# A frequency-domain convolution on one core: weight differences spread over rounds, evictions shared by clocked sums, a third range for one tile, fillers among the last matmuls

## The chip, the core and the metric

The kernel runs on one core of a Trainium2 chip. The core has a matrix engine (TensorE; the profile lists its matmuls as PE and its weight loads as PEld), VectorE (DVE), ScalarE (ACT), GpSimd (POOL) and SyncE (SP, which here only issues transfers). They run side by side and wait for each other on semaphores. The metric is device time in microseconds; a profiled execution has a span besides, from its first to its last instruction.

## The reference: what is computed

```python
# x: (1, 224, 224, 96) bf16, w: (7, 7, 96, 96) bf16
wp = jnp.pad(w, ((0, H - K), (0, W - K), (0, 0), (0, 0)))
Xf = rfft2(x, axes=(1, 2));  Wf = rfft2(wp, axes=(0, 1))
Yf = jnp.einsum('bhwi,hwio->bhwo', Xf, Wf)
y = irfft2(Yf, s=(H, W), axes=(1, 2)).astype(bf16)
```

That is a circular 7x7 convolution of a 224x224 image, with 96 input channels and 96 output channels.

## The kernel before: stages, queues and names

The width is cut into seven tiles of 32 pixels. Along the height the kernel works with short Fourier transforms of length 34 on eight blocks of 28 rows: each block becomes 17 frequency planes (`NS` = 17) of two real parts. Along the width the seven taps stay a direct convolution, with even and odd pixels apart. All matrix work is on PE, in PSUM banks of 512 columns; one pool holds all eight banks, and a bank is free again when it has been evicted (copied to SBUF).

Four kinds of work follow each other for each tile.

- **Forward transform.** Matmuls of the pixels (`xn`, for the first tile `WF`'s late end) with the transform matrix `Fm`; their evictions fill `xf`. Later tiles use `a_jobs` (all 17 planes at once, line 414). The first three tiles use `f_jobs` (line 424), which does the planes in two ranges, `SH2` = (0, 8, 17) (line 41), since the buffer of an earlier tile comes free plane by plane: `xf` has two buffers. A range has one matmul for each pixel, phase and half of the rows, 64 in all, with 2·(planes)·4 columns. `new_xf` (line 363) copies three halo pixels on ACT for each range and phase. `then_load` hangs the load of a later tile's pixels on the last job of a range.
- **Weights.** `prep_jobs(gi)` (line 320) transforms the weights of one group of planes (`PGRP`, line 31): twelve jobs `mk_` of four matmuls (`pb<-wq`, 120 columns each) with one eviction to `WF`, and then, except for the first group, one `diff` a plane (line 350): a DVE subtraction on 96x960 elements, w2 = w0 - w1, the third of the three weight planes that a complex product by three real ones needs. The jobs of a group and its differences form one list.
- **Rounds.** `b_round(t, s)` (line 474) does one plane of one tile. 33 matmuls (`pb<-WF,J` and `pb<-WF,xf`, 96 columns) go to two banks. After the first bank's, ACT makes `tt_` and DVE makes `u`; then the jobs of `mid()` are put in; after the second bank's matmuls DVE makes `v`; and POOL (or DVE, where `ydve`) adds u and v to `yf`, which goes to a scratch tensor in DRAM. The second part of the first bank's weights (slot 2 of the plane) is a difference, so a round's third group of matmuls waits for it. `jit` (line 446) makes the sums and differences `J` of `xf` on DVE for up to three planes ahead.
- **Inverse transform.** `c_jobs` (line 627): the scratch is read back as `tt`; two matmuls a job with the matrix `G` (`pb<-tt,Gm`, 384 columns), each evicted to an output tile (`yo` or a freed `J` buffer) and sent out.

The first two tiles run together, the second four rounds behind (`LAG`), in a loop over r from 0 to 20 (line 739); their rounds share the time with the weights of all groups and with the third tile's forward transform. The remaining tiles run one after the other, with the forward transform of the next and the inverse of the one before between their rounds.

The order is the program's own: every engine runs its instructions in the order in which they are written down. `add(a, b, jobs)` (line 723) gives a list of jobs the slots a to b (two slots a round, so slot k belongs to round k/2), and `pace` (line 707) draws from each list evenly. Every transfer keeps its place too. Almost all instructions are recorded through one helper, so the profile gives L87 for nearly every line; groups are told apart by tile names.

`evac` (line 122) chooses DVE or ACT for an eviction: it keeps a running sum of estimated costs for each (`load["v"]`, `load["a"]`), to which rounds, `jit` and `diff` add their own, and takes the engine whose sum stays lower. The sum of DVE starts at `BIAS` = 3000 (line 703).

**The end** (from line 825). The last tile's scratch is in six parts with own loads (`load_p`); a first block of its inverse (planes 0 to 8, matrix `GA`, function `first`) needs only early parts, the second (`GB`, function `second`) adds the planes from the last three and ends the bank. Seven jobs, 14 matmuls, of the tile before remain and run ahead; then eight `first` matmuls take all eight banks, then `WARM` = 20 matmuls with zeros from the tile `wu` are added to the last bank (line 847), then `second` and `first` alternate, each `second` evicted by DVE and ACT in turn (`tail_evac`) and sent out two by two. The last write to scratch is issued by ACT, and the two loads that wait for the scratch parts by SP ahead of the last output transfers.

Of the kernel before, what the change touches and what calls it, by code (L numbers as in the profile page):

```python
# [14 lines left out]
B = 28  # L15
# [12 lines left out]
NTAP = 10  # L28
# [9 lines left out]
JGB = ((0, 3), (3, 6), (6, 9), (9, 12), (12, 15), (15, 17))  # L38
LAG = 4
CQ = {2: (11, 0), 3: (11, 2), 4: (9, 4), 5: (7, 5), 6: (6, 4)}  # L40
SH2 = (0, 8, 17)
MERGE = ()
NP2 = 0
WARM = 20
BIAS = 3000.0


def slot(s, part):
# [4 lines left out]
def kernel(  # L53
# [7 lines left out]
    _, H, W, C = x.shape  # L61
# [6 lines left out]
    FR = 2 * NS  # L68
# [39 lines left out]
    def bank():  # L108
        return pools["psb"].tile([128, 512], F32, name="pb")

    load = {"v": 0.0, "a": 0.0}
    tail = [0]
    parts = {}

# [7 lines left out]
    def evac(out_ap, in_ap, n):  # L122
        if tail[0]:
            return tail_evac(out_ap, in_ap, n)
        cv, ca = 180 + 1.0 * n, 160 + 0.85 * n
        if load["v"] + cv <= load["a"] + ca:
            load["v"] += cv
            return VE.tensor_copy(out=out_ap, in_=in_ap)
        load["a"] += ca
        return SE.copy(out=out_ap, in_=in_ap)  # L130
# [189 lines left out]
    def prep_jobs(gi):  # L320
        s0, s1 = PGRP[gi]
        ns = s1 - s0
        full = gi == 0
        ncol = (NSLOT_OF(s0, s1) if full else 2 * ns) * NTAP
        nb = C // NB
        hb = NB // 2
        assert NB * ncol <= 512 and C2 % hb == 0

        def mk_(ob):
            def f():  # L330
                pw = bank()
                pv_ = pw[:, 0:NB * ncol].rearrange("p (k h q) -> p k h q", h=2, q=ncol)
                ev = Em[:, :, slot(s0, 0):slot(s1 - 1, 2) + 1, :]
                ev = ev.rearrange("p h a t -> p h (a t)") if full else ev.rearrange("p h (s r) t -> p h s (r t)", r=3)[:, :, :, 0:2 * NTAP]
                for k in range(hb):
                    o = ob * hb + k
                    TE.matmul(pv_[:, k], lhsT=wqx[0:PW2, o:o + 127 * C + 1:C], rhs=ev, start=True, stop=True)
                pv_ = pv_[0:C]
                o0, o1 = ob * hb, (ob + 1) * hb
                wv = WF[0:C, slot(s0, 0):slot(s1 - 1, 2) + 1]  # L340
                if full:
                    wv = wv.rearrange("i a t (h o) -> i (a t) h o", h=2)
                    apart(("W", gi), ob, evac(wv[..., o0:o1], pv_.rearrange("i k h q -> i q h k"), NB * ncol))
                    return
                wv = wv.rearrange("i (s r) t (h o) -> i s (r t) h o", r=3, h=2)
                apart(("W", gi), ob, evac(wv[:, :, 0:2 * NTAP, :, o0:o1],
                      pv_.rearrange("i k h (s q) -> i s q h k", s=ns), NB * ncol))
            return f

        def diff(s):  # L350
            def f():
                load["v"] += 60 + C * NTAP / 1.92
                w0, w1, w2 = (WF[0:C, slot(s, r)].rearrange("i t o -> i (t o)") for r in range(3))
                VE.tensor_tensor(out=w2, in0=w0, in1=w1, op=ALU.subtract)
            return f
        return [mk_(ob) for ob in range(nb)] + ([] if full else [diff(s) for s in range(s0, s1)])

    def NSLOT_OF(s0, s1):
        return slot(s1 - 1, 2) + 1 - slot(s0, 0)
# [24 lines left out]
        apart(("A", t), (pos, jg, ph), evac(xo, pi, m * FR * JG))  # L384

    def a_mm(pa, xb, px, n):
        for k in range(n):
            i = px + 2 * k
            TE.matmul(pa[:, k * FR * JG:(k + 1) * FR * JG], lhsT=xb[:, i * C:i * C + 128],
                      rhs=Fm.rearrange("p r s j -> p (r s j)"), start=True, stop=True)  # L390
# [31 lines left out]
        return jobs  # L422

    def f_jobs(t, part):
        s0, s1 = SH2[part], SH2[part + 1]
        n = 2 * (s1 - s0) * JG
        nr = -(-TW * n // 512)
        e = [-(-TW * i // nr) for i in range(nr + 1)]
        fv = Fm[:, :, s0:s1].rearrange("p r s j -> p r (s j)")

        def mk_(jg, a, b, ph):
            def f():
                pa = bank()
                for k in range(b - a):
                    i = 2 * (a + k) + ph
                    TE.matmul(pa[:, k * n:(k + 1) * n], lhsT=xbuf(t, jg)[:, i * C:i * C + 128], rhs=fv, start=True, stop=True)
                xo = xf_tiles[t][0:C, ph, :, s0:s1, HALO + a:HALO + b, jg * JG:(jg + 1) * JG]
                pi = pa[0:C, 0:(b - a) * n].rearrange("c (w r s j) -> c r s w j", r=2, s=s1 - s0, w=b - a)
                return apart(("A", t), (a, jg, ph, part), evac(xo, pi, (b - a) * n))
            return f  # L440
        return [[mk_(jg, a, b, ph) for a, b in zip(e[:-1], e[1:]) for ph in range(2)] for jg in range(2)]
# [32 lines left out]
    def b_round(t, s, mid, end, ydve=False, planes=()):  # L474
# [14 lines left out]
        def conv(bank, col, m, part, add=False, both=False):  # L489
            pl = st[m][part] if s > 0 else (xv[:, 0, :, 0], Jb[:, 2:4], Jb[:, 0:2])[m][:, part]  # L490
            tp = TAPS[m]
            for k, tp_ in enumerate(tp):
                o, wv = bank[:, col:col + C], WF[0:C, slot(s, part), tp_, :]
                if both:
                    o, wv = bank[:, col:col + 2 * C].rearrange("p (m o) -> p m o", m=2), wv.unsqueeze(1).to_broadcast([C, 2, C])
                TE.matmul(o, lhsT=pl[:, (HALO - k) * NJ:(HALO - k) * NJ + 128], rhs=wv,
                          start=(k == 0 and not add), stop=(k == len(tp) - 1 and not both and m != 2 or not add and not both and k == len(tp) - 1))
# [19 lines left out]
        else:  # L517
# [39 lines left out]
                if last is not None:  # L557
                    tc.add_manual_dep(y.ins, last.ins.name, SYNC, reason="sum after planes")
            load["a"] += 490 if merge else 410
            load["v"] += (560 if ydve else 350 if t < 2 else 0) + (560 if merge else 900)  # L560
            end()
        if s == y1 - 1:
            dst, yo0 = scr_tiles[t], 0
# [63 lines left out]
    def c_jobs(t):  # L627
        jobs = []
        w0 = t * 2 * TW
        for gi, h in LT:  # L630
            hold = {}
            nq = 2 if gi < 2 else 3

            def mk_(q, gi=gi, h=h, nq=nq, hold=hold):
                def put(j0, nj, px, npx, row, col):
                    dma(out[0, j0 * B:(j0 + nj) * B, w0 + px:w0 + px + npx, :].rearrange("h w c -> h (w c)"),
                        hold["yo"][row:row + nj * B, col:col + npx * C])

                def f():
                    if q % 2 == 0:  # L640
                        hold["yo"] = new_yo()
                    tt = tt_tiles[(t, gi, h)]
                    yo = hold["yo"]
                    nj = 2 if q == 2 else 3
                    for b in range(2):
                        pb = bank()[0:nj * B, 0:4 * C]
                        TE.matmul(pb, lhsT=G[0:nj * FR, 0:nj * B],
                                  rhs=tt[0:nj * FR, 4 * q + 2 * b:4 * q + 2 * b + 2, :].rearrange("p w e -> p (w e)"), start=True, stop=True)
                        k = 2 * (q % 2) + b
                        evac(yo[0:nj * B, k * 4 * C:(k + 1) * 4 * C], pb, 4 * C)  # L650
                    if q == 1 and gi < 2:
                        put(gi * 3, 3, h * PXC, PXC, 0, 0)
                    elif q == 1:
                        put(6, 2, 0, 16, 0, 0)
                        for j in range(2):
                            put(6 + j, 1, 24, 8, 2 * B, j * 8 * C)
                    elif q == 2:
                        put(6, 2, 16, 8, 0, 0)
                    if q == nq - 1:
                        held[gi == 2] -= 1  # L660
                        pump()
                return f
            for q in range(nq):
                jobs.append(mk_(q))
# [23 lines left out]
            f()  # L688
    for _ in range(3):
        warm(9)  # L690
    for f in prep_jobs(0):
        f()
    last = [f() for f in fj[0][1]]
    for jg in range(2):
# [5 lines left out]
    stmp_cm.__exit__(None, None, None)  # L700
    yf_pool = ctx.enter_context(tc.tile_pool(name="yf", bufs=YBUF))
    tv_pool = ctx.enter_context(tc.tile_pool(name="tv", bufs=2))
    load["v"], load["a"] = BIAS, 0.0

    t_pool = t2_pool = yo_pool = None

# [17 lines left out]
        qs.append([a, b, jobs, len(jobs)])  # L724

    for gi in range(1, len(PGRP)):
        add(2 * PGRP[gi - 1][0], 2 * PGRP[gi - 1][1] - 1, prep_jobs(gi))
    for t in range(2):
        scr_tiles[t] = dr_pool.tile([TW, NJ, NS, 4 * C], BF16, name="scr")
    bursts = {}  # L730
# [8 lines left out]
    for r in range(NS + LAG):  # L739
        if r == 0:  # L740
            add(0, 4, fj[1][1])
        for p in range(2):
            if r == (1, 3)[p]:
                new_xf(1, SH2[p], SH2[p + 1])
                fj = f_jobs(1, p)
                if p == 1:
                    for jg in range(2):
                        fj[jg][-1] = then_load(fj[jg][-1], 2, jg)
                add(2 * r + 1, 2 * r + (5, 8)[p], fj[0] + fj[1])
        for p in range(2):  # L750
            if r == (9, 17)[p]:
                new_xf(2, SH2[p], SH2[p + 1])
                fj = f_jobs(2, p)
                if p == 1:
                    for jg in range(2):
                        fj[jg][-1] = then_load(fj[jg][-1], 3, jg)
                add(2 * r, 2 * r + (10, 6)[p], fj[0] + fj[1])
        if r == PGRP[-2][1] + 1:
            assert not any(q[2] for q in qs[:len(PGRP) - 1])
            wtmp_cm.__exit__(None, None, None)  # L760
            t_pool = ctx.enter_context(tc.tile_pool(name="tt", bufs=NTT, side="right"))
            t2_pool = ctx.enter_context(tc.tile_pool(name="tt2", bufs=1, side="right"))
# [130 lines left out]
```

## Time and profile before

| | |
|---|---|
| time, median of 5 runs | 277.16 us (275.04 to 280.5) |
| profiled execution: time, span | 278.79 us, 277.1 us |
| PE busy, PEld busy | 261.0 us (94%), 238.3 us (86%) |
| DVE, ACT, POOL busy | 221.9, 195.3, 98.0 us |
| bytes moved | 46.76 MB, mean 169 GB/s |
| granted TensorE clock, mean | 0.986 |
| chain that ended last | PE 59%, DVE 13%, issue 8%, DMA 7%, ACT 6% |

The page is of one execution. "Busy" sums the time with at least one instruction in work; matmuls overlap, so a busy PE is not a PE at its peak. A row of the timeline gives the start, the duration, the engine, the operation with output and input, and in brackets the engine's idle time before it with what ended it; neighbouring instructions of the same kind are merged into one row with their number (x12). A number such as 0.50 for the clock is the share of full speed that was granted. The stages that matter below are: up to 18 us loads and tables; 18 to about 104 us the first two tiles with the weights; to 257 us the other tiles; then the end.

### The profile page before, as it was taken

What the parts mean: (1) busy time and instruction counts of PE and PEld (TensorE: products, weight loads), DVE (VectorE), ACT (ScalarE), POOL (GpSimd) and SP (SyncE); (2) the same over time, 40 slices, a digit from 0 to 9 for tenths busy, and PEclk for the clock granted to TensorE, in tenths of its full rate; (3) what the DMA queues carried; (4) which work ended last, traced back from release to release, by engine and by line L of the source; (5) the groups of instructions that cost most, each with busy time, mean ns of one, the idle gap of its engine ahead of it and who ended that gap; (6) DMA issues with size and microseconds to landing.
All of it is one profiled execution on the core that took longest, in us unless ns stands there. A gap on an engine that the chain in (4) does not pass through costs nothing.

```text
span 277.1 us, 11903 instructions
## 1 busy us (share of the span) xinstructions
PE 261.0 (94%) x5018; PEld 238.3 (86%) x5018; DVE 221.9 (80%) x464; ACT 195.3 (70%) x478; POOL 98.0 (35%) x146
## 2 busy tenths in 40 slices
PE   8969898999999899999999999999999999988893
PEld 3649898999999898899999999999999999978572
DVE  5528789998979869977977897888988799988923
ACT  5428896859782676897988879887988864445413
POOL 7720022246446553233243224223323416323000
PEclk9998999999999999999999999999999999999989
DMA  7945213151111199995969487777957642898656
GB/s 186 211 113 148 67 47 107 45 150 47 45 48 67 71 285 148 259 280 158 306 186 260 124 233 210 204 228 181 309 167 192 198 154 89 200 237 245 191 160 195
DMA packets 46609, 46.76 MB, mean 169 GB/s; under 512 B 35274, under 2 KB 37974, under 8 KB 46458
## 3 DMA queue, kind: packets, MB, share of 16 engines
q1 hardware_dynamic: 45692, 44.34, 58.1%
q10 hardware_dynamic: 864, 1.67, 1.8%
q8 instruction: 39, 0.64, 1.0%
q14 instruction: 14, 0.11, 0.1%
HBM read 24.65 MB, written 21.33 MB: 166 GB/s over the span
## 4 chain that ended last, share of the span: by engine, by line
PE 59%; DVE 13%; issue 8%; DMA 7%; ACT 6%; POOL 3%; SPq 1%; DVEq 0%; ACTq 0%
PE pb L87 59%; DMA wq<-in_w_dram 5%; DVE J L87 4%; DVE v L87 3%; POOL yf L87 3%; DVE WF L87 2%; DMA out_dram<-J 2%; ACT WF L87 2%; ACT xf L87 2%; DVE u L87 2%; DVE yf L87 1%; SPq L87 1%; ACT J L87 1%; DVE yo L87 0%; DVE xf L87 0%
## 5 line engine op out<-in xcount | busy, mean ns | idle before, releaser
L87 PE MATMUL pb<-WF,J 96*128 96x96 bf16 x2898 | 166.2, 206 | 5.1 <-ACT yo L87 1.4
L87 PEld LDWEIGHTS <-J 96*128 96x128 bf16 x2898 | 141.7, 98 | 14.1 <-issue 5.3
L87 POOL TENSOR_TENSOR yf<-v,u 128x384 bf16<-128x384 f32 x85 | 84.6, 1012 | 147.3 <-issue 100.4
L87 ACT CAST xf<-pb 96x408 bf16<-96x408 f32 (+4 forms) x146 | 68.1, 494 | 8.2 <-PE pb L87 4.8
L87 PE MATMUL pb<-WF,xf 96*128 96x96 bf16 x952 | 60.2, 206 | 1.6 <-DVE WF L87 1.2
L87 DVE TENSOR_TENSOR J<-xf 96x1824 bf16<-96x1824 bf16 (+1 forms) x84 | 59.2, 744 | 0.1
L87 PEld LDWEIGHTS <-xf 96*128 96x128 bf16 x952 | 47.1, 98 | 2.1 <-issue 1.7
L87 PE MATMUL pb<-Fm,xn 118*128 118x136 bf16 (+2 forms) x512 | 43.0, 208 | 0.2 <-DVE u L87 0.2
L87 ACT CAST WF<-pb 96x480 bf16<-96x480 f32 (+1 forms) x59 | 29.2, 577 | 8.2 <-PE pb L87 8.1
L87 PE MATMUL pb<-tt,Gm 102*84 102x384 bf16 (+1 forms) x132 | 32.3, 326 | 1.2 <-DVE yo L87 0.7
L87 ACT CAST yo<-pb 84x384 bf16<-84x384 f32 (+1 forms) x62 | 26.6, 483 | 5.9 <-PE pb L87 3.8
L87 ACT CAST J<-pb 84x384 bf16<-84x384 f32 (+1 forms) x63 | 27.1, 487 | 4.6 <-DMA tt<-scr 2.6
L87 PEld LDWEIGHTS <-xn 118*128 118x128 bf16 x512 | 27.8, 98 | 0.6 <-issue 0.4
L87 DVE TENSOR_TENSOR J<-J 96x912 bf16<-96x912 bf16 (+1 forms) x42 | 25.0, 595 | 0.0
L87 PE MATMUL pb<-wq 98*128 98x120 bf16 (+1 forms) x288 | 22.0, 230 | 2.3 <-DMA wq<-in_w_dram 2.3
L87 PEld LDWEIGHTS <-wq 98*128 98x128 bf16 x288 | 20.0, 150 | 2.8 <-issue 2.7
L87 PE MATMUL pb<-wu 128*128 128x512 bf16 (+1 forms) x64 | 16.9, 431 | 1.0 <-DVE ct L87 1.0
L87 DVE TENSOR_TENSOR yf<-v,u 128x384 bf16<-128x384 f32 x27 | 15.7, 580 | 0.9
L87 PEld LDWEIGHTS <-wu 128*128 128x128 bf16 (+1 forms) x64 | 8.1, 128 | 9.0 <-issue 3.5
L87 DVE CAST WF<-pb 96x480 bf16<-96x480 f32 (+1 forms) x13 | 7.5, 610 | 8.2 <-PE pb L87 8.1
L87 PEld LDWEIGHTS <-Gm 102*84 102x84 bf16 (+1 forms) x132 | 11.3, 117 | 3.1 <-issue 2.2
L87 DVE TENSOR_TENSOR WF<-WF 96x960 bf16<-96x960 bf16 x15 | 10.9, 777 | 0.0
(393 smaller groups left out, 233.7 us busy)
## 6 DMA issues: line engine op xcount, KB each, us to landing
scr<-yf SPq DMA_DIRECT2D x30, 288.0 KB
xn<-in_x_dram SPq DMA_DIRECT2D x12, 672.0 KB
tt<-scr SPq DMA_DIRECT2D x24, 336.0 KB
out_dram<-yo SPq DMA_DIRECT2D x12, 252.0 KB
out_dram<-J SPq DMA_DIRECT2D x12, 252.0 KB
tt<-scr SPq DMA_DIRECT2D x6, 288.0 KB
wq<-in_w_dram SPq DMA_DIRECT2D x1, 1719.0 KB
scrl<-yf ACTq DMA_DIRECT2D x5, 288.0 KB
```

Source lines behind the costliest of these rows:

```text
L87: r = fn(*a, **k)
```

## The change

It has five parts.

1. `prep_jobs` returns the weight jobs and the differences apart. The jobs keep the group's slots; each difference gets its own slot, 2(s - 1) for plane s, the middle of the round before the one that uses it.
2. The sums of `evac` get a clock: `load["p"]` adds up an estimate of PE's time wherever matmuls are written down, and both sums are raised to it before each choice. Some estimates change too (a difference 250 + 500 for 60 + 500; a round on POOL 150 for 350), and `BIAS` is 2000.
3. `SH2` becomes a table by tile. The third tile's planes are done in three ranges (0, 8, 13, 17), begun in rounds 9, 14 and 17, in place of two begun in 9 and 17.
4. Behind each of the 14 inverse matmuls at the end stands one matmul with zeros into the same bank (384 columns), which ends the bank's accumulation.
5. `WARM` is 12 in place of 20.

```diff
-SH2 = (0, 8, 17)
+SH2 = {0: (0, 8, 17), 1: (0, 8, 17), 2: (0, 8, 13, 17)}
...
-WARM = 20
-BIAS = 3000.0
+WARM = 12
+BIAS = 2000.0
...
         cv, ca = 180 + 1.0 * n, 160 + 0.85 * n
+        for k in "va":
+            load[k] = max(load[k], load["p"])
         if load["v"] + cv <= load["a"] + ca:
...
-                load["v"] += 60 + C * NTAP / 1.92
+                load["v"] += 250 + C * NTAP / 1.92
...
-        return [mk_(ob) for ob in range(nb)] + ([] if full else [diff(s) for s in range(s0, s1)])
+        return [mk_(ob) for ob in range(nb)], [] if full else [diff(s) for s in range(s0, s1)]
...
+                load["p"] += max(26.0, 0.43 * n) * (b - a)
...
+            load["p"] += 42.5 * len(tp)
...
-            load["v"] += (560 if ydve else 350 if t < 2 else 0) + (560 if merge else 900)
+            load["v"] += (560 if ydve else 150 if t < 2 else 0) + (560 if merge else 900)
...
                         TE.matmul(pb, lhsT=G[0:nj * FR, 0:nj * B],
-                                  rhs=..., start=True, stop=True)
+                                  rhs=..., start=True, stop=not tail[0])
+                        if tail[0]:
+                            TE.matmul(pb.rearrange("p (a b) -> p a b", a=3), lhsT=wu[:, 0:nj * B], rhs=wu[:].unsqueeze(1).to_broadcast([128, 3, 128]),
+                                      start=False, stop=True)
...
-        add(2 * PGRP[gi - 1][0], 2 * PGRP[gi - 1][1] - 1, prep_jobs(gi))
+        pj, dj = prep_jobs(gi)
+        add(2 * PGRP[gi - 1][0], 2 * PGRP[gi - 1][1] - 1, pj)
+        for i, f in enumerate(dj):
+            k = 2 * (PGRP[gi][0] + i) - 2
+            add(k, k + 1, [f])
...
-        for p in range(2):
-            if r == (9, 17)[p]:
-                new_xf(2, SH2[p], SH2[p + 1])
+        for p in range(3):
+            if r == (9, 14, 17)[p]:
+                new_xf(2, SH2[2][p], SH2[2][p + 1])
                 fj = f_jobs(2, p)
-                if p == 1:
+                if p == 2:
...
-                add(2 * r, 2 * r + (10, 6)[p], fj[0] + fj[1])
+                add(2 * r, 2 * r + (8, 7, 5)[p], fj[0] + fj[1])
```

More of the change, by code (lines that the diff above doesn't have):

```diff
@@ L109, in bank @@
         return pools["psb"].tile([128, 512], F32, name="pb")
-    load = {"v": 0.0, "a": 0.0}
+    load = {"v": 0.0, "a": 0.0, "p": 0.0}
     tail = [0]
@@ L334, in f @@
                 ev = ev.rearrange("p h a t -> p h (a t)") if full else ev.rearrange("p h (s r) t -> p h s (r t)", r=3)[:, :, :, 0:2 * NTAP]
+                load["p"] += 63.0 * hb
                 for k in range(hb):
@@ L386, in a_mm @@
     def a_mm(pa, xb, px, n):
+        load["p"] += 59.0 * n
         for k in range(n):
@@ L424, in f_jobs @@
     def f_jobs(t, part):
-        s0, s1 = SH2[part], SH2[part + 1]
+        s0, s1 = SH2[t][part], SH2[t][part + 1]
         n = 2 * (s1 - s0) * JG
@@ L646, in f @@
                         pb = bank()[0:nj * B, 0:4 * C]
+                        load["p"] += 166.0
                         TE.matmul(pb, lhsT=G[0:nj * FR, 0:nj * B],
-                                  rhs=tt[0:nj * FR, 4 * q + 2 * b:4 * q + 2 * b + 2, :].rearrange("p w e -> p (w e)"), start=True, stop=True)
+                                  rhs=tt[0:nj * FR, 4 * q + 2 * b:4 * q + 2 * b + 2, :].rearrange("p w e -> p (w e)"), start=True, stop=not tail[0])
+                        if tail[0]:
+                            TE.matmul(pb.rearrange("p (a b) -> p a b", a=3), lhsT=wu[:, 0:nj * B], rhs=wu[:].unsqueeze(1).to_broadcast([128, 3, 128]),
+                                      start=False, stop=True)
                         k = 2 * (q % 2) + b
@@ L690 @@
         warm(9)
-    for f in prep_jobs(0):
+    for f in prep_jobs(0)[0]:
         f()
@@ L702 @@
     tv_pool = ctx.enter_context(tc.tile_pool(name="tv", bufs=2))
-    load["v"], load["a"] = BIAS, 0.0
+    load["v"], load["a"], load["p"] = BIAS, 0.0, 0.0
     t_pool = t2_pool = yo_pool = None
@@ L743 @@
             if r == (1, 3)[p]:
-                new_xf(1, SH2[p], SH2[p + 1])
+                new_xf(1, SH2[1][p], SH2[1][p + 1])
                 fj = f_jobs(1, p)
@@ L749 @@
                 add(2 * r + 1, 2 * r + (5, 8)[p], fj[0] + fj[1])
-        for p in range(2):
-            if r == (9, 17)[p]:
-                new_xf(2, SH2[p], SH2[p + 1])
+        for p in range(3):
+            if r == (9, 14, 17)[p]:
+                new_xf(2, SH2[2][p], SH2[2][p + 1])
                 fj = f_jobs(2, p)
-                if p == 1:
+                if p == 2:
                     for jg in range(2):
                         fj[jg][-1] = then_load(fj[jg][-1], 3, jg)
-                add(2 * r, 2 * r + (10, 6)[p], fj[0] + fj[1])
+                add(2 * r, 2 * r + (8, 7, 5)[p], fj[0] + fj[1])
         if r == PGRP[-2][1] + 1:
-            assert not any(q[2] for q in qs[:len(PGRP) - 1])
+            assert not any(q[2] for q in qs[:4 * len(PGRP) - 8])
             wtmp_cm.__exit__(None, None, None)
```

## The prediction

> **What bounds the kernel now.** I read four views in this order: the table of busy time by stage, the waits of the matrix engine (PE), the timelines of the stretches where PE waits, and the fine table of the last 20 us. By stage (start:end, length, then busy us of PE, PEld, DVE, ACT, POOL, the granted PE clock, DMA share, GB/s):
>
> ```profile
> 24.00:34.00 10.00, 9.01 (x187) 8.71 (x186) 8.07 (x15) 8.78 (x22) 0.37 (x1) 1.00 0.54 145
> 34.00:50.00 16.00, 14.38 (x324) 14.02 (x321) 15.25 (x28) 13.30 (x33) 4.01 (x4) 1.00 0.23 67
> ...
> 112.00:238.00 126.00, 125.86 (x2536) 118.31 (x2533) 106.38 (x223) 103.88 (x265) 44.14 (x44) 1.00 0.73 209
> ...
> 262.00:268.00 6.00, 5.96 (x28) 4.19 (x27) 1.06 (x3) 0.95 (x3) 0.00 (x0) 0.72 0.81 225
> ```
>
> From 112 to 238 us PE is busy for 125.86 of 126 us: nothing that moves work between DVE and ACT is worth anything there. The change must earn its keep ahead of 112 us, where PE is idle for 10-9.01 + 16-14.38 = 2.6 us up to 50 us and, by the same table, 0.8 us in 80:93 (PE 12.22 of 13, DVE 11.38), and in the tail. PE's waits ahead of 112 us, apart from the first load, are 1.9 us on "DVE WF" in three pieces, 1.4 on "DVE u", 1.3 on "DVE J". The largest piece, DVE and then PE:
>
> ```profile
> 43.31 2.54 DVE L87 TENSOR_TENSOR WF<-WF 96x960 bf16<-96x960 bf16 x3
> 45.77 0.54 DVE L87 SCALAR_TENSOR_TENSOR v<-tt__944,pb 128x384 f32<-128x384 f32 x1
> ...
> 44.76 0.33 PE L87 MATMUL pb<-WF,xf 96*128 96x96 bf16 x4 [1.02 <-DVE WF L87]
> ```
>
> Three weight differences stand in one clump of 2.54 us; PE waits 1.02 us for the first, and v, which frees the sum on POOL, is queued behind all three. In the tail:
>
> ```profile
> 259.74 1.01 DVE L87 CAST yo<-pb 84x384 bf16<-84x384 f32 x2
> ...
> 262.06 1.00 DVE L87 CAST yo<-pb 84x384 bf16<-84x384 f32 x2
> ...
> 263.94 4.38 PE L87 MATMUL pb<-wu 128*112 128x384 bf16 x20
> ...
> 268.15 0.98 PE L87 MATMUL pb<-xf,GB 128*112 128x384 bf16 x5
> 268.51 4.47 DVE L87 CAST tt<-pb 112x384 bf16<-112x384 f32 x8 [5.45 <-PE pb L87]
> ```
>
> The 20 fillers on zeros (wu) take 4.38 us, and the last real matmuls (GB) begin the moment they end; DVE has waited 5.45 us. Are the fillers hiding a load? They run before the last part of the last tile (32 rows, 192 KB) must have arrived. Its write to scratch is issued by ACT at 259.85 and has landed when SP issues the read, about 261.8: 1.95 us. The read is as large, so it lands near 264.0. PE therefore has about 4 us of fillers too many. The clock in the same stretch:
>
> ```profile
> 261.50:262.00 0.50, 0.50 (x4) 0.29 (x3) 0.50 (x2) 0.50 (x2) 0.00 (x0) 1.00 0.03 8
> ...
> 262.50:263.00 0.50, 0.50 (x4) 0.30 (x3) 0.50 (x2) 0.45 (x2) 0.00 (x0) 0.50 0.99 273
> ...
> 266.00:266.50 0.50, 0.50 (x5) 0.39 (x4) 0.00 (x0) 0.00 (x0) 0.00 (x0) 1.00 0.86 258
> ```
>
> After the loosely filled stretch of inverse matmuls (257 to 262, PE busy 3.80 of 5 us) the clock falls to 0.50 until about 265.7, so first eight and most fillers run at half speed.
>
> **The tail, worked out.** The inverse matmuls left at the end are 14, each with one evacuation, 7 to an engine; DVE cannot begin them before its last yf ends (259.74), and they end at 263.06 (262.06 + 1.00). A filler behind each adds 14 x 0.163 us (from the 0.33 us of a pair spaced at 0.165) = 2.3 us of PE work and delays each evacuation by one filler; but eight PSUM banks let eight pairs run ahead of 259.74, and the other six pairs (6 x 0.33 = 2.0 us) are released from 260.3 on, so each is ready before its evacuation's turn. Cost nothing; if that lead were gone, one filler and its drain, 0.3 us. The eight "first" matmuls need the freed banks: the last can start after 263.06 and ends near 263.45. Twelve fillers at full clock: 12 x 0.163 = 1.95 us, so the GB matmuls start at 265.4, later than the landing at 264.0, and 2.75 us earlier than 268.15. From there everything is as before (24 matmuls, 16 evacuations, eight output transfers), but those transfers now meet the earlier outputs, which hold the DMA engines until about 267.2 (225 GB/s over 262:268); 8 x 172 KB at some 275 GB/s end near 272.3, against 270.97 + 1.9 by the issues (last issue ends 273.72 now). I take 0.15 us off: **-2.6**.
>
> [...] Full clock gives -2.6; half clock throughout gives 263.06 + 0.4 + 12 x 0.325 = 267.4, or -0.8. PE's share rises from 3.8 to nearly all of the first eight pairs and two thirds after; I take full clock.
>
> **Differences one per round.** The 15 differences remain (642 ns each, up to 1401 beside POOL); each now stands alone between u and v in the round before its own. Round 2's first use waits for the first difference as before, but ACT has one 360-column evacuation (0.51 us) less ahead of it, so the 0.74 us wait shrinks by about 0.5; the 1.02 at 44.76 goes; of the 0.44 us at 86.35 (a J held up behind the clump at 81.74, 2.13 us) most goes. Together 1.9 us. What is late next: DVE is full in 34:50 (15.25 of 16), evacuation work there stays, and "DVE u" keeps its 0.52 at 49.52. I keep three quarters: **-1.5**. Bounds: 0, if the stretch is simply the two engines' total work; -3.4, all idle of 24:50 and 80:93. Each v waits 0.64 us behind a difference in 15 rounds instead of about 2 us in five; POOL has room (44 of 126 us).
>
> **Clocked sums.** They only choose the engine. In the order of the changed program DVE has three evacuations more than before (xf 17 for 14, yo 5 for 4, WF 6 for 7), and after 112 us only two change engine. Three of 0.5 us, hidden under a full PE or in DVE's idle fifth: **0**; if that cover is gone, 0.5 us each, 1.5 us.
>
> **Third tile in three ranges.** Its 128 forward matmuls (64 and 72 columns) become 192 (64, 40, 32), the evacuations stay 20 (8+8+4), two ACT halo copies are added (0.16 us of fixed cost each, hidden: ACT is busy 4.76 of 13 us in 80:93). Rows: 16 matmuls of 64 columns take 0.63 us, so (0.63-0.193)/15 = 29.1 ns apart; 12 of 72 columns take 0.56, or 33.0. In proportion to columns, 40 and 32 would cost 64 x (18.2+14.6) = 2.1 us, no more than the 64 x 33.0 = 2.1 now. [...] No row is narrower than 64 columns; between 25 and 29.1 I take 27: 3.5 us, **+1.4** of PE work. Where it falls: the 40-column range sits in rounds 14 to 16 (83 to 93 us), where PE's round takes 1.60 us (83.11 to 92.69, six rounds) for 33 x 42.6 ns = 1.40 us of matmuls, because DVE sets the pace; 1.2 us of slack swallow most of its 1.7 us. The stretch after it, 93 to 100, loses 0.4 us, and the 1.42 us in which ACT waited at 101.01 to evacuate the third tile goes, and with it a good part of the 0.52 us that PE waits for J at 105.84. The fourth tile's pixel load hangs on the last of these jobs and stands one place earlier in SP's queue, ahead of a scratch write (98.91 now) that is not read for many rounds; its pixels are first used at 104.03, so the swap costs nothing, and 0.7 us of SP's issue if the write mattered. Net **0** (from -0.7 to +1.4).
>
> **Sum.** -2.6 - 1.5 + 0 + 0 = -4.1 us against the profiled execution: span 277.1 to 273.0, time 278.79 to 274.7. The runs' median is 277.16, 1.6 below the profiled one; I set the same difference against it: **273.1 us**.
>
> **Rivals.**
> 1. The first stage is bound by the total work of DVE and ACT, not by its clumps: gain there 0, and the third range costs 0.5: -2.1, 275.1. For it: DVE 15.25 and ACT 13.30 of 16 us; against: ACT sat idle 2.70 us at 43.73 to 46.43 waiting for PE.
> 2. The clock falls in spite of the fillers: tail -0.8, sum -2.3, 274.9. For it: the six later pairs still come at the pace of the evacuations.
> 3. All idle goes, and PE alone bounds from 24 us: -2.6 - 3.4 + 0.4 = -5.6, 271.6.
> 4. Slower: narrow matmuls are held by their weight loads. Each loads 128 columns anew (98 ns a load, overlapped today). [...] It decides from (2.1+1.2+4.1)/128 = 58 ns a pair. [...]
>
> **How the numbers follow.** Chances: forecast 0.48, rival 1 0.18, rival 2 0.12, rival 3 0.12, rival 4 0.10. One per cent (2.8 us, about what a measurement of this kernel can tell from no change) puts the bounds at 274.4 and 279.9. The forecast with its own range (271.8 to 274.6) is nearly always below the first; rivals 1 and 2 lie just above it and fall under it one time in four, given the 275.0 to 280.5 that runs spread now; rival 3 is below. That makes faster 0.64, same 0.28, slower 0.08. The range reaches from rival 3's lower side to above rivals 1 and 2: 270.3 to 276.7.
>
> **What would show it.** Tail: PE clock 1.00 in 262 to 266, GB matmuls some 2 us after the last wu, starting about 2.3 us after DVE's last yo evacuation (5.1 now). First stage: no "DVE WF" wait over 0.4 us, and 112 us (the third tile's first inverse matmul) reached 1 to 2 us earlier. Third tile: 32-column matmuls spaced 25 to 29 ns, rounds 14 to 16 still near 1.6 us. I am wrong if the clock shows 0.50 again, if PE idles before the GB matmuls for the load, or if "DVE u" waits replace those on WF.

## The result, and the profile after

The changed kernel takes 277.52 us (median of 36 runs, 274.61 to 280.57), the kernel before beside it 277.99 (71 runs, 274.57 to 285.3). The ratio is 1.0001 [0.9981, 1.0022]: no change. (Medians here are over all runs; the ratios leave disturbed runs out, so the two differ a little.) The forecast of 273.1 us was wrong, and its range ended 0.8 us below the result. The profiled execution of the changed kernel has a time of 279.02 us and a span of 277.2, against 278.79 and 277.1. The two profiles are not alike in clock: it is 0.50 in before from 20.12 to 23.53 and in the tail from 262.46 to 265.88, in the changed kernel from 19.86 to 26.68 and from 241.72 to 245.14.

These are the rows by stage that answer to the four shown of before (length, then busy us of PE, PEld, DVE, ACT, POOL, then clock, DMA share, GB/s), from the changed kernel:

```profile
24.00:34.00 10.00, 9.76 (x191) 9.62 (x189) 8.12 (x16) 8.41 (x20) 0.00 (x0) 0.87 0.42 118
34.00:50.00 16.00, 15.42 (x346) 15.07 (x343) 15.39 (x31) 13.97 (x35) 5.94 (x6) 1.00 0.23 68
112.00:238.00 126.00, 125.83 (x2534) 118.24 (x2532) 106.65 (x225) 101.63 (x258) 44.17 (x44) 1.00 0.74 209
262.00:268.00 6.00, 5.82 (x35) 4.09 (x34) 2.91 (x7) 2.83 (x7) 0.00 (x0) 1.00 0.75 199
```

PE is fuller up to 50 us (15.42 for 14.38 in the second row), and the tail has its full clock (1.00 for 0.72). Both are what was wanted; where did the time go? To find the place I compared the starts of all 119 `tt_`, one a round, each counted from the first weight matmul (the first weights arrive at 16.9 to 18.9 us, which differs from run to run and is nobody's doing). Changed minus before: -1.34 us at the 13th round, +1.27 at the 27th, +0.96 from the 41st to the 105th, +3.24 at the 107th, +2.81 at the last. So a gain in the first rounds is lost before round 27, and 2.3 us more go near 237 us; 1.3 of these are back at the 110th (+1.95), and 0.9 go again by the last, after the second stretch at half clock. The longer half clock at the start lies ahead of the 13th round. The kernel c4 below is the same program up to its last fillers and has none there: it stands at -3.87 at the 13th and at -1.25 at the 27th, so the 2.6 us lost between the two are no matter of the clock. The tail then gives 1.7 us back: from the last `tt_` to the end it is 17.7 us for 19.4.

The first loss, in the changed kernel's timeline (start, duration, engine, operation, output and input):

```profile
57.66 1.73 DVE L87 TENSOR_TENSOR J<-xf 96x1824 bf16<-96x1824 bf16 x2
59.31 0.62 DVE L87 TENSOR_TENSOR J<-J 96x912 bf16<-96x912 bf16 x1
59.86 0.34 DVE L87 SCALAR_TENSOR_TENSOR u<-pb,tt__1431 128x192 f32<-128x192 f32 x1
60.07 1.00 POOL L87 TENSOR_TENSOR yf<-v,u 128x384 bf16<-128x384 f32 x1 [1.95 <-issue]
60.13 1.45 DVE L87 TENSOR_TENSOR WF<-WF 96x960 bf16<-96x960 bf16 x1
61.50 0.54 DVE L87 SCALAR_TENSOR_TENSOR v<-tt__1431,pb 128x384 f32<-128x384 f32 x1
61.63 0.33 PE L87 MATMUL pb<-WF,xf 96*128 96x96 bf16 x4 [0.78 <-DVE WF L87]
```

The lone difference at 60.13 takes 1.45 us, and PE waits 0.78 us for it. It begins 0.06 us after a sum on POOL that ends at 61.07, and 61.07 + 0.51 = 61.58 is its end: nearly all of its own 0.64 us is done after the sum. Ten of the fifteen lone differences are drawn out in this way by a running sum, and each ends 0.51 to 0.52 us after it. Is the difference too long, or only too late for PE? PE came for this one at 60.85 (61.63 - 0.78); had it lasted 0.64 us, it would have ended at 60.77. The other long wait, 0.88 us at 87.09, reads the same: PE came at 86.21, and the difference begun at 85.59 would have ended at 86.23. So some 1.6 of PE's 2.4 us on differences come from their length. The other way round, POOL stood still for 1.95 us while DVE made the J: the v that its sum adds was done at 57.74, but the sum began at 60.07, 0.1 us after the last J. In these rows the two engines take turns. The groups of the two kernels (count, then busy us, mean ns, idle before), before and then changed:

```profile
L87 DVE TENSOR_TENSOR WF<-WF 96x960 bf16<-96x960 bf16 x15 | 10.9, 777 | 0.0
```

```profile
L87 DVE TENSOR_TENSOR WF<-WF 96x960 bf16<-96x960 bf16 x15 | 15.8, 1055 | 0.2
```

The same fifteen subtractions cost 4.9 us more of DVE. In before's five clumps of three only the first meets a running sum: it takes 0.99 to 1.40 us in four clumps and 0.65 in the one without a sum, and the ten behind take 0.64 to 0.65. In those four the next sum on POOL, which waits for the v behind the clump, begins 0.54 us after the clump's end.

The second loss, near 237 us (SPq and ACTq are issues of transfers):

```profile
233.05 1.22 SPq L87 DMA_DIRECT2D out_dram<-J  x3
234.37 0.33 SPq L87 DMA_DIRECT2D out_dram<-yo  x1
234.89 4.40 SPq L87 DMA_DIRECT2D tt<-scr  x6
237.99 0.34 ACTq L87 DMA_DIRECT2D scrl<-yf  x1
238.71 0.85 ACT L87 CAST yo<-pb 84x384 bf16<-84x384 f32 x2 [4.08 <-DMA tt<-scr]
239.23 0.70 PE L87 MATMUL pb<-tt,Gm 102*84 102x384 bf16 x2 [1.26 <-ACT yo L87]
```

The program makes ACT's issue of a scratch write wait for an earlier transfer whose completion counter it uses, the third `out_dram<-J`; that wait ends at 237.94, and ACT's evictions queue behind the issue (ACT idle for 4.08 us). The chain of waits names it (start, us, what): it has landed 4.0 us after its start. POOL's sums, for which the write waits too, were done at 236.20.

```profile
233.90 4.01 DMA out_dram<-J
```

The records of its counter have every increment but one by 235.78, 1.88 us after the issue, and the last at 237.91. In before the same issue stood at 236.01, when POOL's sums were done, and ACT waited 2.02 us, for PE.

### The profile page after: what moved, and what is told of

It is laid out like the page before. It is cut to its first block, busy times and chain, and to the rows that moved or that the text cites. A ratio compares the mean times of both kernels' runs of the same rounds, so it can differ in the third digit from the quotient of the medians.

```text
span 277.2 us, 12048 instructions
## 1 busy us (share of the span) xinstructions
PE 264.1 (95%) x5088; PEld 241.9 (87%) x5088; DVE 227.2 (82%) x467; ACT 196.2 (71%) x477; POOL 99.8 (36%) x146
## 4 chain that ended last, share of the span: by engine, by line
PE 63%; DVE 14%; issue 8%; DMA 6%; ACT 3%; POOL 3%; SPq 1%; DVEq 0%; ACTq 0%
PE pb L87 63%; DVE J L87 5%; DMA wq<-in_w_dram 5%; DVE WF L87 4%; POOL yf L87 3%; DVE v L87 2%; DVE u L87 2%; DMA out_dram<-J 1%; SPq L87 1%; ACT xf L87 1%; ACT WF L87 1%; DVE yf L87 1%; ACT yo L87 1%; DVE tt L87 0%; DVEq L902 0%
## 5 line engine op out<-in xcount | busy, mean ns | idle before, releaser
L87 PE MATMUL pb<-WF,J 96*128 96x96 bf16 x2898 | 168.7, 207 | 1.4 <-ACT yo L87 0.4
L87 POOL TENSOR_TENSOR yf<-v,u 128x384 bf16<-128x384 f32 x85 | 86.4, 1032 | 148.5 <-issue 98.3
L87 ACT CAST xf<-pb 96x408 bf16<-96x408 f32 (+5 forms) x143 | 67.1, 490 | 7.8 <-PE pb L87 5.7
L87 PE MATMUL pb<-WF,xf 96*128 96x96 bf16 x952 | 61.7, 207 | 2.6 <-DVE WF L87 2.1
L87 PE MATMUL pb<-Fm,xn 118*128 118x136 bf16 (+4 forms) x576 | 44.4, 203 | 0.0
L87 PE MATMUL pb<-tt,Gm 102*84 102x384 bf16 (+1 forms) x132 | 34.1, 330 | 1.3 <-ACT yo L87 1.3
L87 PE MATMUL pb<-wu 128*128 128x512 bf16 (+3 forms) x70 | 19.1, 403 | 1.0 <-DVE ct L87 1.0
L87 DVE TENSOR_TENSOR WF<-WF 96x960 bf16<-96x960 bf16 x15 | 15.8, 1055 | 0.2
L87 PEld LDWEIGHTS <-wu 128*128 128x128 bf16 (+3 forms) x70 | 8.0, 116 | 8.8 <-issue 3.5
L87 DVE CAST WF<-pb 96x400 bf16<-96x400 f32 (+1 forms) x12 | 7.0, 609 | 7.3 <-PE pb L87 7.1
```

Source lines behind the costliest of these rows:

```text
L87: r = fn(*a, **k)
```

## The experiments

Each run records its span and mean granted clock. The clock explains a good part of the scatter: over the 177 runs behind the ratios below, a fit with one constant for each kernel, one for each group of runs, and one slope gives 0.64 ± 0.10 us of span for each us of lost clock, (1 - clock) x span, and leaves a scatter of 0.8 us. "At equal clock" below is the difference from before by this fit. Over all 245 runs the slope is 0.88 ± 0.07; c1 then comes out 1.1 us lower, the others move by 0.6 us or less, and no sign changes.

| kernel | median us | ratio to before | at equal clock, us |
|---|---|---|---|
| a1_clumps: changed, differences in clumps | 275.47 | 0.9905 [0.9864, 0.9945] | -2.4 ± 0.6 |
| b1_tail: before + fillers and `WARM` 12 | 276.50 | 0.9965 [0.9936, 0.9994] | -0.3 ± 0.4 |
| b2_diffs: before + one difference per round | 279.70 | 1.0018 [0.9979, 1.0056] | +1.4 ± 0.6 |
| b3_range: before + third range | 278.79 | 0.9992 [0.9961, 1.0024] | -0.4 ± 0.5 |
| c1_after_v: changed, difference behind v | 285.45 | 1.0218 [1.0151, 1.0285] | +6.0 ± 0.8 |
| c2_sums: before + clocked sums | 277.11 | 0.9933 [0.9901, 0.9965] | -1.0 ± 0.6 |
| c3_late: a1 + late evictions as before | 274.92 | 0.9840 [0.9784, 0.9896] | -2.7 ± 0.8 |
| c4_warm: changed, `WARM` 4 | 276.85 | 0.9965 [0.9929, 1.0000] | -0.4 ± 0.6 |
| d1_lead: changed, difference behind v, earlier | 275.58 | 0.9926 [0.9899, 0.9953] | -2.7 ± 0.8 |
| d2_lead_late: d1 + late evictions as before | 274.11 | 0.9877 [0.9830, 0.9923] | -2.8 ± 0.8 |

Before had medians of 278.14 beside a and b, 279.43 beside c, 278.11 beside d. The changed kernel has no row, since no clock is on record for the runs of before beside it; c4 stands for it, as the same program but for eight fillers.

**a1_clumps.** One part undone:

```diff
-        for i, f in enumerate(dj):
-            k = 2 * (PGRP[gi][0] + i) - 2
-            add(k, k + 1, [f])
+        add(2 * PGRP[gi - 1][0], 2 * PGRP[gi - 1][1] - 1, pj + dj)
```

> The changed kernel with its differences put back into one clump of three at the end of each group's list. If lone differences are what costs (beside a sum on POOL they take 1.17 to 1.46 us, in a clump only the first does), their mean falls from 1055 to near 780 ns, round 28 comes some 1.5 us earlier counted from the first weight matmul, and the time is 1 to 2 us below the changed kernel and below before (276). If the third range is what costs, nothing changes against the changed kernel (277.5).

The ratio falls from 1.0001 to 0.9905: lone differences cost the changed kernel 2.7 us by the ratios, and 2.0 at equal clock by c4 (-0.4) against a1 (-2.4). In the profile a1's rounds stand at -1.85 us against before from the 41st on, where the changed kernel's stand at +0.96, a part of it for its 3.4 us more of half clock; mean of a difference 772 ns.

**b1_tail, b2_diffs, b3_range.** One part each, put into the kernel before, with the edits of the change itself.

> The kernel before with the end's two edits alone (fillers behind the 14 inverse matmuls, 12 for 20 behind the first eight). If the end gains what the two traces show (last yf to the end 15.6 us after the change, 17.3 before), the time is 1.5 to 2 us below before (275.8). If it is given back in the output transfers or the last load, it is within 0.5 us of before.

> The kernel before with one difference per round alone. If lone differences cost, their mean is above 1000 ns and the time is 0.5 to 1.5 us above before, with a gain up to round 12 and a loss from there to round 28. If the prediction's step was right, 1.5 us below before.

> The kernel before with the third tile's forward in three ranges alone. By the prediction 0 (within 0.7 us of before); if the third range is what ate the gain, 1 to 2 us above before, with the loss in rounds 24 to 33.

The tail gives 1.0 us (ratio 0.9965), between the two outcomes named; but little of it (0.3 ± 0.4) at equal clock: mean lost clock falls from 3.2 us in before to 2.2, which at 0.64 is the other 0.7. Lone differences are no gain even alone: their mean is 1096 ns here too, and PE's waits on "DVE WF" from 24 to 104 us rise from 1.9 us in three pieces to 4.8 in seven. The third range is free, as expected.

**c2_sums.** The edits of `evac`, its estimates and `BIAS`, put into the kernel before.

> The kernel before with the clocked sums alone (new costs and the start of DVE's sum with them). Theory, from the rounds of the changed kernel with its clumps back: the first seven rounds gain 1.4 us because fewer evictions stand on ACT ahead of tt_, and it is kept: 276.5, ratio 0.995. Since no eviction of the last tiles changes engine here, no wait of 4 us for the transfers near round 104. The prediction's own price: no difference from before (1.000).

A gain, where I had priced nothing. Its source is in before's timeline and in that of a1:

```profile
29.89 0.48 ACT L87 ACTIVATE tt__604<-pb 128x288 f32<-128x288 f32 x1
30.40 0.36 DVE L87 SCALAR_TENSOR_TENSOR u<-pb,tt__604 128x192 f32<-128x192 f32 x1 [1.74 <-ACT tt__604 L87]
31.93 0.33 PE L87 MATMUL pb<-WF,J 96*128 96x96 bf16 x4 [0.74 <-DVE WF L87]
```

ACT is behind with evictions, so `tt_` is late, DVE stands idle for 1.74 us, and its difference comes late for PE. Rows of 10 us at the same distance from the first weight matmul show the shift, before and then a1:

```profile
28.35:38.35 10.00, 9.01 (x206) 8.71 (x203) 7.84 (x15) 9.12 (x23) 1.91 (x2) 1.00 0.11 30
```

```profile
26.94:36.94 10.00, 9.56 (x223) 9.46 (x221) 9.74 (x20) 9.64 (x24) 2.02 (x2) 1.00 0.13 40
```

DVE works 9.74 of 10 us for 7.84, and the waits of 1.74 and 0.74 us are gone. Whether a lone difference costs more on top of the sums (2.7 us by the ratios) than alone (1.4 ± 0.6) stays open. Profiles with as much half clock at the start suggest that it hardly does: at the 41st round b2 stands 1.87 us behind before, the changed kernel 2.24 behind d1 below, and c4 2.11 behind d2.

**c1_after_v.** The difference of plane s moves from between u and v to behind v, in the round before its own:

```diff
-            add(k, k + 1, [f])
+            dq[PGRP[gi][0] + i - 1] = f
```

> The changed kernel, each difference still alone in its round but placed behind v (ahead of the evictions that follow v) instead of between u and v. Theory (DVE's subtraction and POOL's sum take turns: the one that begins first holds the other off for its whole length): here the difference begins the moment v ends, before POOL can begin the sum that v releases, so each lasts 0.64 to 0.70 us, the fifteen together about 10 us where the changed kernel has 15.8, and POOL's sum begins late instead. The first stage gains what the clump gained, 2.5 to 3 us: 274.5 to 275.5. Rival (both are merely slowed by sharing, or DVE has no room for a lone difference anywhere): differences stay near 1.05 us on average, POOL's sums stretch over 1.0, and the time stays at 277 to 278.

Half of the theory held. The differences are short: half of them at most 648 ns, none over 1021, mean 720 ns. But the kernel is the slowest of all:

```profile
41.87 1.40 DVE L87 TENSOR_TENSOR J<-xf 96x1824 bf16<-96x1824 bf16 x2
43.19 0.62 DVE L87 TENSOR_TENSOR J<-J 96x912 bf16<-96x912 bf16 x1
43.74 0.65 DVE L87 TENSOR_TENSOR WF<-WF 96x960 bf16<-96x960 bf16 x1
43.89 1.35 POOL L87 TENSOR_TENSOR yf<-v,u 128x384 bf16<-128x384 f32 x1 [5.72 <-DVE J L87]
44.44 0.43 PE L87 MATMUL pb<-WF,xf 96*128 96x96 bf16 x4 [2.76 <-DVE WF L87]
```

Where a round makes J, the J stand between v and the difference, and the next round needs it at once: PE waits 8.8 us for differences in six pieces, 2.76 here. I had moved the difference past three instructions and not asked who waits. POOL's row shows the turn-taking from its side: begun 0.15 us after the difference, the sum needs 1.35 us for its 1.0.

**d1_lead.** The same place behind v, but at least one whole round of the other tile lies between a difference and its use; the first three stay a clump. With k for the plane, a difference is now kept by round and tile:

```diff
+            dq[(k - 1, 0) if i < 2 else (k - 2, 1)] = f
```

> The changed kernel, with the first three differences back in one clump and the other twelve alone, each right behind a v, and at least one whole other round between it and its use (behind v of the round that ends one or two rounds of the pair of tiles earlier, never with sums J in between). Theory (the loss of lone differences is the turn-taking of DVE and POOL, and the loss of the first version behind v is only that each was used at once): the twelve last 0.64 to 0.70 us, PE has no wait on them, and the time is that of the kernel with clumps or up to 1 us better: 274.5 to 275.5 where before has 277 to 278, ratio 0.985 to 0.992. Rival (a lone difference costs about what it did, wherever it stands, since it then holds POOL off and the sums come late): 277 to 278, ratio 0.998 to 1.002.

```profile
L87 DVE TENSOR_TENSOR WF<-WF 96x960 bf16<-96x960 bf16 x15 | 10.8, 732 | 0.1
...
69.35 0.65 DVE L87 TENSOR_TENSOR WF<-WF 96x960 bf16<-96x960 bf16 x1
69.52 1.35 POOL L87 TENSOR_TENSOR yf<-v,u 128x384 bf16<-128x384 f32 x1 [0.40 <-DVE v L87]
```

The twelve lone differences are still lone, they last 0.64 to 1.02 us, seven of them 0.65, and PE's waits on WF are 1.4 us, about 1.0 of it one piece. So it is not being alone that costs. The ratio is 0.9926 where the changed kernel has 1.0001. Against the changed kernel with as much lost clock at the start (7 us at half clock in both), its 41st round is 2.24 us earlier. It is not better than the clumps, only as good. d1 changes two things at once, the place and the lead, and no kernel was run with the lead alone; that the length does the harm in the changed kernel is read from the rows at 61.63 and 87.09 above, and that a short difference without lead does harm too from c1.

**c3_late and d2_lead_late.** Did the late loss come from two evictions that the new sums give to DVE near 220 us (in a1 and d1 two of `yo`, in the changed kernel and c4 one of `xf` and one of `yo`)? Both kernels set the sums at the third tile so that all later choices are those of before:

```diff
+    load["v"], load["a"], load["p"] = 85901.7, 68653.2, -1e12
```

> The changed kernel with the differences back in clumps, and from the third tile on with the engines for evictions that the kernel before chose (two yo evictions go back from DVE to ACT). Theory A (those two evictions bring the wait of ACT for a transfer near round 104, 2.25 us): it goes, 273.3, ratio to before 0.983, and 2.2 us below the kernel with clumps. Theory B (the wait comes from how late a small output transfer lands, which the evictions don't decide): it stays, 275.5.

> The kernel just described, with the engines of the kernel before for evictions from the third tile on. Theory (gains add): 0.5 us or less from the second edit, since the long wait near round 104 came and went between runs of one program: ratio 0.983 to 0.990. Rival (the two evictions decide that wait): 2 us below the kernel just described, ratio 0.978 to 0.983, and no wait of 4 us near round 104 in this one but one in the other.

They don't. In c3, without those two evictions on DVE, ACT still waits 3.64 us there and PE 0.61 and 0.36 (it has the time back four rounds later, ahead of a wait that is there anyway). In d1 and c4, which have them, PE waits 0.25 us at most. The same rows in c4:

```profile
229.21 1.22 SPq L87 DMA_DIRECT2D out_dram<-J  x3
230.89 0.32 SPq L87 DMA_DIRECT2D out_dram<-yo  x1
231.39 6.06 SPq L87 DMA_DIRECT2D tt<-scr  x6
233.40 0.34 ACTq L87 DMA_DIRECT2D scrl<-yf  x1
234.13 0.85 ACT L87 CAST yo<-pb 84x384 bf16<-84x384 f32 x2 [2.33 <-DMA tt<-scr]
```

ACT's issue stands where POOL's sums end (233.37), as in before; the third transfer, issued at 230.06, had its last increment at 231.88. Over all twelve profiles that transfer takes either 1.8 to 2.0 us (eight of them) or 3.9 to 4.0 (the changed kernel, a1, c1 and c3), and in each of the four a single increment comes late. Why it does stays open. The wait alone left nothing behind in c3 (-1.88 us against before at the 106th round, -1.85 at the last); in the changed kernel and in a1 3.4 us of half clock follow within 3 us, and 1.6 us stay. That PE's longer wait there (1.2 us in one piece) brings the half clock on is not shown: before has one of 1.37 us at 250.37, and none follows.

The ratios of the two (0.984, 0.9877) overlap those of a1 and d1, and at equal clock all four lie within 0.4 us: c3's ratio is where Theory A had it, though the wait stayed. The ratios of all four lie below those of both kernels; c3 and d2 have the lowest medians, 274.92 and 274.11.

**c4_warm.** `WARM` 4 in place of 12.

> The changed kernel with 4 fillers in place of 12 ahead of the last matmuls. Theory (the last load's landing sets the end): PE idles about 1.3 us longer, the GB matmuls start as before, 8.4 us after the last tt_, and the time is that of the changed kernel within 0.4 us. The prediction's view (fillers set the start): the GB matmuls start 1.3 us earlier and the time falls by as much. Third way: PE's clock falls for want of work and the end is 1 to 2 us later.

```profile
257.06 0.33 ACTq L87 DMA_DIRECT2D scrl<-yf  x1
...
260.96 0.82 PE L87 MATMUL pb<-wu 128*112 128x384 bf16 x4
...
263.33 0.99 PE L87 MATMUL pb<-xf,GB 128*112 128x384 bf16 x5 [1.56 <-DMA xf<-scrl]
```

Now PE waits openly for the last load, 1.56 us, and the GB matmuls start 8.44 us after the last `tt_` (8.36 in the changed kernel, where the fillers end only 0.2 us ahead of GB). The load sets the start, not the fillers: it lands 6.3 us after the issue of the write that it waits for.

## Why the prediction was wrong, step by step

**Differences one per round, forecast -1.5, measured +1.4 ± 0.6 alone and +2.7 (by the ratios) on top of the sums.** This is the failed step: "The 15 differences remain (642 ns each, up to 1401 beside POOL)". I had the 1401 ns in hand and priced all fifteen at 642, and I wrote that POOL has room, which is beside the point: what counts is when a sum runs. A difference between u and v stands where POOL has just been released by the last v. The sum is 1.0 us, so a difference that meets it in full costs up to 1.6 as an estimate (the longest seen is 1.46), and v, which releases the next sum, is queued behind. Before's own profile showed it:

```profile
43.20 0.99 POOL L87 TENSOR_TENSOR yf<-v,u 128x384 bf16<-128x384 f32 x1 [4.74 <-DVE J L87]
```

The clump that the prediction shows, at 43.31, begins 0.11 us after this sum, and its first difference is the one of 1401 ns. PE came for it at 43.74 (44.76 - 1.02); at 0.64 us it would have ended at 43.95. So about 0.8 of the 1.02 us that I put down to the clump were the sum's, and spreading the clump did not take them away: b2 waits 1.08 us at 44.57. The rows fit, within 0.15 us, a difference and a sum done one after the other: at 60.13 in the changed kernel 0.94 us of the sum were left and the difference alone is 0.64, 1.58 for the 1.45 seen; in c1 the difference had 0.50 left and the sum is 1.00, 1.50 for 1.35. (Where the two begin within 0.04 us, at 34.99 and 35.02 in the changed kernel, it is the later one, the difference, that goes first, and the sum takes 1.58.) As an estimate from the sum's measured 1.0 us, each of the fifteen could have cost up to 1.0 us more, 15 us of DVE where I allowed none; it was 4.9. v is not drawn out: it takes 0.54 us beside a sum (at 57.20 in the changed kernel) as without one (61.50).

**Tail, forecast -2.6, measured -1.0, of which -0.3 ± 0.4 at equal clock.** The mechanism, that fillers hold the clock at 1.00, fits the profiles; two sizes were off. First, "lands near 264.0" in before, 4.15 us after ACT's issue: c4 shows 6.3, which sets the start of GB (the later of the two reads is issued at 259.55 and takes 3.8 us, where 2.2 were allowed). Second, and larger, I took the clock's fall in one execution for a property of the program. Old tail, from the last `tt_` to GB: 8.90 us in b3 and 8.96 in c2, where the clock stayed at 1.00; 10.44 in before and 11.84 in b2, where it was 0.50 for 3.4 and 6.8 us. New tail: 8.0 to 8.9 in all eight profiles, and in none did it fall there; none of eight against two of four speaks for the fillers but does not prove them. Between executions without a fall GB starts 0.6 us earlier (8.4 on average); the rest is a fall that came in two of four. The outputs gave back a little: GB to the end is 9.2 us on average for 9.0.

**Clocked sums, forecast 0 (at worst 1.5 lost), measured -1.0 ± 0.6.** I counted what three more evictions cost DVE and found room for them. I did not count what ACT, without them, does earlier: `tt_`, for which DVE stood idle. In c2 DVE has only one eviction more in all, but two that were ACT's (of `WF` at 24.31, of `xf` at 26.98) now lie on DVE ahead of that `tt_`, and u waits 0.16 us for it instead of 1.74. The 1.74 us was in the waits of DVE, which I had not read.

**Third range, forecast 0, measured -0.4 ± 0.5.** Right: b3 stands 0.35 us behind before at the 27th round and 0.43 ahead of it from the 41st, a small loss and a gain after it, as the steps had it. The narrow matmuls:

```profile
83.11 0.56 PE L87 MATMUL pb<-Fm,xn 118*128 118x40 bf16 x16
...
94.35 0.76 PE L87 MATMUL pb<-Fm,xn 118*128 118x40 bf16 x24
95.55 0.56 PE L87 MATMUL pb<-Fm,xn 118*128 118x32 bf16 x16
```

One lasts 0.18 us, so they are (0.76 - 0.18)/23 = 25.2 ns apart, 25.3 for 32 columns: 40 and 32 cost the same, where proportion to columns had 18.2 and 14.6, and 128 of them 3.2 us, not 3.5. No row of before shows the 25 ns that the step set against 29.1 to take 27; the changed kernel's rows show 25.2 and 25.3. Rival 4 needed 58 ns. The two added halo copies cost ACT 0.29 us together (0.67 + 0.61 for the pairs of two ranges, 0.99 for the pair of one in before), about the 0.16 us each that the step put down.

**The sum.** The parts measured alone come to -0.35 + 0.18 - 0.08 - 0.67 = -0.9% (each ± 0.3 to 0.4, so ± 0.7 together); in one kernel they gave 0.0 ± 0.2. A higher price of the differences on top of the sums would close the gap, and so would the late transfer near 237 us if it came often there; neither is shown. Three signs of a wrong forecast were named: clock at 0.50 did not come in the tail, PE's wait for the load did once fillers were fewer (c4), and the "DVE u" waits did not return but those on WF did, 2.4 us in five pieces. No rival named turn-taking; the one slower rival, narrow matmuls held by their weight loads, did not come.

## What to carry to other kernels

Before you spread a clump of VectorE work, look up what GpSimd does at each new place, and price the operation by its slowest row beside GpSimd (here 1.40 us in before, where it is 0.64 alone). A thing moved to a later place in a queue needs a round of lead over its user (here PE's waits on differences were 8.8 us without it and 1.4 with it). Don't size a saving by a clock fall that one execution shows: look for it in more executions first.

## What the runs showed of the hardware

In the twelve profiles half clock comes in pieces of one length. The stretches at 0.50 ahead of the final output wait last 3.4 us (3.41 or 3.42) or twice that (6.82 or 6.83), and their starts within one execution lie whole numbers of 3.413 us apart: 71 of them from 20.12 to 262.46 in before, 65 from 19.86 to 241.72 in the changed kernel, 64 from 18.92 to 237.38 in a1. One program has none in one execution (c4, d2 up to the end) and 6.8 us at the start in another (the changed kernel, 19.86 to 26.68; d1, 20.94 to 27.77). A stretch need not be idle ahead of it: in before PE was busy for 3.80 of the 5 us from 257 to 262, with no wait over 0.73 us, and the clock fell at 262.46. The fit puts 0.64 us of span on each us lost. What brings a stretch on, no run shows.

The runs of one kernel spread widely here, b2's seventeen over 8.9 us and those of before beside them over 11.6, more than any part of this change is worth: b2's ratio (1.0018 [0.9979, 1.0056]) does not tell its cost from nothing, and the clock beside each time does.
